# Re-spacing interleaved attention stages, moving partial sums and one late weight sum in a fused attention and expert kernel

## The chip, the cores and the metric

The kernel runs on one core of one Trainium2 chip. The metric is the device time of one execution in microseconds (us), the smaller the better. The granted clock of a run is the mean share of full speed that TensorE was allowed in it; 1.000 means that its profile shows no throttled stretch. TensorE is the matmul engine, VectorE and ScalarE the two elementwise engines, GpSimd the fourth, and the sync engine here only issues DMAs.

## The reference

Four batches of block attention (8 heads, 768 positions, 64 wide, 8 blocks), in which keys and values are first mixed between blocks by a matrix from five rounds of row and column normalization. Then a mixture of four experts over all 3072 tokens.

```python
def _attn_ref(q, k, v, sort_net):
    ...                                   # P: five rounds of exp and normalization of sort_net
    k_sorted = einsum('bhij,bhjcd->bhicd', P, k_b)
    v_sorted = einsum('bhij,bhjcd->bhicd', P, v_b)
    ...                                   # per block: softmax(q k^T / 8) v
def _moe_ref(x, domain_probs, w1, w2):
    p = domain_probs / (domain_probs.sum(-1, keepdims=True) + 1e-09)
    for e in range(E):
        h = np.maximum(x @ w1[e], 0.0)
        out += p[:, e:e + 1] * (h @ w2[e])
```

## The kernel before

The expert part works on chunks of 256 tokens, three to a batch. "Chunk (b, c)" is chunk c of batch b. A chunk has a **first layer** (for each expert 2 x 16 matmuls of 256 columns, each half evicted by VectorE) and a **product part**, seven products of a Strassen-like second layer, each a chain over the experts. The products are named b11, b21, t1, t2, n4, t3 and b22, and need sums of the hidden values (`h_sums`). The six chunks of batches 2 and 3, the **last chunks**, use the seven-product scheme in the first layer too, and their weight sums are prepared in batch 1's chunks.

While the experts of batch 0 run, the attention of batch 1 is computed in between, and batches 2 and 3 follow inside the rest of batch 0 and batch 1. A list says at which chunk and at which place (slot) in it each attention stage is issued:

```python
PLANS = {
    0: [ ...                         # (chunk, slot, stage, batch, pair of heads)
        (2, 7, st_a, 1, 3), (2, 8, st_x, 1, 3), (2, 9, st_v, 2, 0),
        (2, 9, st_q, 2, 0), (2, 10, st_v, 2, 1), (2, 11, st_k, 2, 0), (2, 11, st_lv, 3, 0), (2, 12, st_q, 2, 1),
        (2, 12, st_bk, 2, 1),
    ],
    1: [
        (0, 0, st_s, 2, 0), (0, 0, st_q, 2, 2), (0, 1, st_v, 2, 2), ...
        (1, 11, st_x, 3, 0), (1, 12, st_s, 3, 2), (1, 13, st_s, 3, 3), (1, 13, st_x, 3, 1), (1, 14, st_a, 3, 2),
        (2, 0, st_a, 3, 3), (2, 0, st_x, 3, 2), (2, 2, st_x, 3, 3),
    ],
}
```

Everything on `nc.sync` stands in one queue, in program order: query transposes, the copies of the mixed values, output transposes and the stores of the results.

```python
att = ctx.enter_context(tc.tile_pool(name="att", bufs=2))

def st_v(b, pr):                     # value mix
    ...                              # 2 matmuls, then ScalarE casts into vo
    if pr % 2:
        for r in range(R):           # six copies
            nc.sync.dma_start(vs[...], vo[...])

def st_q(b, pr):                     # query transpose
    qT = att.tile([P, R, P], F16, name=f"qT_{b}_{pr}", tag="qT", bufs=3)
    nc.sync.dma_start_transpose(qT[:], ...)

def st_s(b, pr):                     # scores: 16 matmuls with kT and qT, then 2 exponentials on ScalarE
    ...
def st_a(b, pr):                     # weighted sum, then VectorE normalizes 2 heads
    xsl = att.tile([P, NB, 2, D], F16, name=f"xsl_{b}_{pr}", tag="xsl")[0:BLK]      # 2 buffers
    ...
def st_x(b, pr):                     # output transpose: the input of the experts
    nc.sync.dma_start_transpose(xTs[b][:, pr], xsls[(b, pr)]...)
```

The first layer, and the product part of a last chunk:

```python
def chunk_first(b, c, es, first, slot):
    for e in es:
        for g in range(2):
            ps = psm(...)                                    # 2 buffers
            ...                                              # 16 matmuls
            nc.vector.scalar_tensor_tensor(out=Hb[...], in0=ps[:], ...)     # eviction
            if e > first:
                for w in ((1,), (2, 3))[g]:
                    h_sums(e - 1, w)
            slot()

def last_chunk(...):
    ...
        tt(oa1, bankB, p1[:], ALU.add)
        for e in range(E - 1):
            h_sums(e, 2)
        product(bankC, blk(1, 1), "n4")
        nc.scalar.copy(ob1, bankC)
        h_sums(E - 1, 1)
        h_sums(E - 1, 2)
        for e in range(E):
            h_sums(e, 4)
        product(bankQ, sm(0), "t1")          # needs the first sum of every expert
```

The softmax here doesn't subtract the row's maximum and nothing guards it: scores larger than these inputs give would overflow.

## Time and profile before

| | before |
|---|---|
| time, median of the first 3 runs (range) | 370.25 us (370.07 to 370.59) |
| span of the profiled run | 368.1 us |
| TensorE busy | 356.6 us (97%) |
| granted clock | 0.998 (half rate in the last 1.1 us alone) |

The question is *where* in the span a wait arises, so the most useful view is the table by stretch. Its columns are the stretch, its length, then the busy time and the number of instructions of TensorE, weight loads, VectorE, ScalarE and GpSimd, then the granted clock (1.00 is full), the DMA share and GB/s. I cut it at the first matmul of each chunk. These are chunk 2 of batch 0 and the three chunks of batch 1:

```profile
core 0: us, PE busy (x) PEld busy (x) DVE busy (x) ACT busy (x) POOL busy (x), PEclk, DMA share, GB/s
...
95.98:118.94 22.96, 22.89 (x247) 19.77 (x244) 19.75 (x39) 6.28 (x12) 3.14 (x4) 1.00 1.16 127
118.94:151.31 32.37, 32.06 (x378) 27.77 (x376) 22.31 (x42) 15.59 (x28) 8.82 (x11) 1.00 1.28 162
151.31:185.63 34.32, 33.44 (x400) 28.54 (x398) 26.52 (x50) 18.30 (x32) 0.00 (x0) 1.00 0.60 104
185.63:211.56 25.93, 25.42 (x247) 22.47 (x244) 24.01 (x46) 1.49 (x4) 0.00 (x0) 1.00 0.22 54
```

The first row has hardly a gap: 22.89 of 22.96 us are TensorE. The others leave 0.3 to 0.9 us each.

### The profile page before, as it was taken

How to read it: one execution, taken by the hardware profiler on the slowest of the kernel's cores; microseconds unless marked ns; L12 is line 12 of the kernel's file. 1: busy time of each engine (PE TensorE's matmuls, PEld its weight loads, DVE VectorE, ACT ScalarE, POOL GpSimd, SP SyncE). 2: the span in 40 equal slices, each digit the busy share in tenths (PEclk: the TensorE clock that was granted, in tenths of full speed). 3: DMA queues.
4: the chain of work that ended last, by engine and by line, in shares of the span. 5: the costliest groups of instructions: out<-in, count | busy, mean ns of one | idle time of the engine just before them, and what ended most of it. 6: DMA issues, size and time to landing. Idle time of an engine off the chain costs nothing.

```text
span 368.1 us, 10549 instructions
## 1 busy us (share of the span) xinstructions
PE 356.6 (97%) x4517; PEld 314.3 (85%) x4517; DVE 280.3 (76%) x558; ACT 157.6 (43%) x282; POOL 117.4 (32%) x134
## 2 busy tenths in 40 slices
PE   8799999998999999999999999999999999999996
PEld 8685858877888888878888899899898998998985
DVE  5654798767898686678789769868779679587694
ACT  2664330543233553256510157165283381561740
POOL 8872111841300152000000018137055082180470
PEclk9999999999999999999999999999999999999999
DMA  7999999999998999652750110310301101102101
GB/s 101 207 208 229 209 209 199 202 192 189 184 110 114 189 172 163 126 118 67 81 124 2 57 59 4 57 59 4 86 30 51 67 3 59 60 2 61 57 16 43
DMA packets 69753, 38.34 MB, mean 104 GB/s; under 512 B 40390, under 2 KB 64716, under 8 KB 69708
## 3 DMA queue, kind: packets, MB, share of 16 engines
q0 software_dynamic: 34640, 17.83, 38.5%
q1 hardware_dynamic: 35068, 19.85, 26.4%
q8 instruction: 35, 0.57, 0.6%
q14 instruction: 10, 0.08, 0.1%
HBM read 42.00 MB, written 6.34 MB: 131 GB/s over the span
## 4 chain that ended last, share of the span: by engine, by line
PE 73%; DVE 12%; DMA 7%; ACT 3%; issue 2%; POOL 2%; DVEq 0%; ACTq 0%; POOLq 0%
PE ps_Q L1114 15%; PE ps_h L766 14%; PE ps_p L751 11%; PE ps_X L1025 8%; PE ps_Q L1025 6%; PE ps_Z L1025 5%; DVE Sb L737 4%; PE ps_h L659 3%; DMA arena<-in_v_dram 3%; PE ps_o L694 3%; DMA qT<-arena 2%; DMA arena<-in_q_dram 2%; DVE Sb L739 2%; ACT kT L396 2%; DVE xsl L423 2%
## 5 line engine op out<-in xcount | busy, mean ns | idle before, releaser
L1038 POOL TENSOR_TENSOR Hb<-tmp,pb 128x512 f16<-128x512 f32 x48 | 61.9, 1295 | 153.3 <-ACT tmp L1037 151.3
L766 PE MATMUL ps_h<-xT,w 128*128 128x256 f16 x672 | 78.7, 273 | 0.5 <-DVE Hb L772 0.5
L766 PEld LDWEIGHTS <-w 128*128 128x128 f16 x672 | 64.5, 98 | 9.5 <-issue 0.7
L772 DVE SCALAR_TENSOR_TENSOR Hb<-ps_h,pb 128x1024 f16<-128x1024 f32 x42 | 51.2, 1222 | 17.1 <-PE ps_h L766 17.1
L1025 PEld LDWEIGHTS <-w 128*128 128x128 f16 x768 | 46.6, 98 | 1.0 <-issue 0.3
L1114 PEld LDWEIGHTS <-Sb 128*128 128x128 f16 x384 | 36.7, 98 | 6.7 <-DVE Sb L737 2.7
L1025 PEld LDWEIGHTS <-arena 128*128 128x128 f16 x576 | 34.7, 98 | 0.2
L1037 ACT ACTIVATE tmp<-tmp 128x512 f32<-128x512 f32 x48 | 30.5, 635 | 6.4 <-DVE tmp L1069 5.2
L751 PEld LDWEIGHTS <-Sb 128*128 128x128 f16 x288 | 27.5, 98 | 3.7 <-issue 0.2
L396 ACT CAST kT<-ps_k 64x384 f16<-64x384 f32 x48 | 22.8, 474 | 17.2 <-PE ps_k L387 16.3
L1114 PEld LDWEIGHTS <-Hb 128*128 128x128 f16 x288 | 27.4, 98 | 2.8
L1025 PE MATMUL ps_X<-kT,arena 128*128 128x128 f16 x384 | 29.3, 219 | 0.0
L121 POOL DMA_DIRECT2D arena<-in_q_dram x24 | 19.9, 837 | 25.0 <-DMA qT<-arena 14.9
L1114 PE MATMUL ps_Q<-w,Sb 128*128 128x256 f16 x192 | 25.8, 273 | 1.0 <-DVE Sb L737 1.0
L737 DVE TENSOR_TENSOR Sb<-Hb 128x512 f16<-128x512 f16 x45 | 26.4, 607 | 0.0
L1061 DVE TENSOR_TENSOR tmp<-ps_Q,tmp 128x512 f32<-128x512 f32 x24 | 16.6, 691 | 12.7 <-ACT tmp L1060 8.5
L413 ACT ACTIVATE ET<-ps_s 96x768 f16<-96x768 f32 x24 | 18.1, 802 | 17.9 <-PE ps_s L406 17.8
L1114 PE MATMUL ps_Q<-w,Hb 128*128 128x256 f16 x192 | 23.9, 273 | 0.0
L1045 ACT COPY ps_X<-ps_Z 128x512 f32<-128x512 f32 x24 | 13.7, 570 | 23.1 <-PE ps_Z L1025 22.5
L1114 PE MATMUL ps_Q<-T,Sb 128*128 128x256 f16 x192 | 22.9, 273 | 0.0
L751 PEld LDWEIGHTS <-Hb 128*128 128x128 f16 x216 | 20.4, 98 | 2.9 <-issue 0.3
L1052 ACT COPY tmp<-ps_X 128x512 f32<-128x512 f32 x24 | 14.1, 587 | 12.2 <-PE ps_X L1025 12.2
(188 smaller groups left out, 607.5 us busy)
## 6 DMA issues: line engine op xcount, KB each, us to landing
w<-in_moe_w_dram POOLq DMA_DIRECT2D x7, 1024.0 KB, 27.4
pb<-p_dram SPq DMA_DIRECT2D x12, 512.0 KB, 6.1
arena<-in_k_dram POOLq DMA_DIRECT2D x8, 384.0 KB, 8.3
arena<-in_v_dram POOLq DMA_DIRECT2D x8, 384.0 KB, 8.8
vs<-arena SPq DMA_DIRECT2D x36, 66.0 KB, 5.4
arena<-in_q_dram POOLq DMA_DIRECT2D x24, 96.0 KB, 7.8
out_dram<-ob SPq DMA_DIRECT2D x9, 256.0 KB, 2.0
out_dram<-oa SPq DMA_DIRECT2D x8, 256.0 KB, 2.5
```

Of the source, the lines that this page charges most:

```text
L121: nc.gpsimd.dma_start(t[:, h // 2, :, h % 2, :], q[b, h].rearrange("(t p) d -> p t d", p=P))
L396: nc.scalar.copy(kT[ds(D * hh, D), r], pk[ds(D * r, D), hh].rearrange("p a (i c) -> p a i c", c=CP),)
L413: nc.scalar.activation(ETs[2 * (pr % 2) + hh][:, 0:S].rearrange("c (a x) -> c a x", a=2), pss[hh][0:BLK, :, 0:HS], AF.Exp, bias=0.0, scale ...
L737: tt(sm[0], blk(0, 1), blk(1, 1), ALU.add)
L751: nc.tensor.matmul(ps, lhs(e, f), Ts[e][rhs][:, f, :], start=(first and e == es[0] and f == 0), stop=(done and e == es[-1] and f == KH - 1 ...
L766: nc.tensor.matmul(ps[:, f, :], w1sb[e][:, kc, ds((4 * g + f) * P, P)], xT[:, kc, ds(2 * c * P, 2 * P)], start=(kc == 0), stop=(kc == NKC ...
L772: nc.vector.scalar_tensor_tensor(out=Hb[:, e, ds(4 * g, 4), :], in0=ps[:], scalar=0.0, op0=ALU.max, in1=pb[:, ds(e, 1), :].broadcast_to([P ...
L1025: nc.tensor.matmul(dst[:, ds(f * P, P)], a[lhs][:, k, ds(f * P, P)], t[rhs][:, k, :], start=(first and f == 0 and k == 0), stop=(f == KH - ...
L1037: nc.scalar.activation(src, src, AF.Relu, bias=0.0, scale=1.0)
L1038: nc.gpsimd.tensor_tensor(Hb[:, e, ds(i * KH, KH), ds(j * P, P)], src.rearrange("p (f x) -> p f x", f=KH), pb[:, ds(e, 1), ds(j * P, P)].b ...
L1061: tt(t22, Q, u3, ALU.add)
L1114: nc.tensor.matmul(ps, lhs(e, f), Ts[e][rhs][:, f, :], start=(first and e == 0 and f == 0), stop=(e == E - 1 and f == KH - 1), skip_group_ ...
```

## The change

Its intent is to space the attention stages so that what one stage hands to the next is ready when TensorE gets there, and to take VectorE work out of the places where TensorE waits for VectorE. Four parts, with no instruction added or removed:

1. `PLANS` re-spaced in all chunks from chunk 1 of batch 0 on.
2. In batch 1's chunks the third sums move from the first layer to the product part.
3. In the six last chunks the first sum of expert 3 goes ahead of the second sums.
4. The order of the weight sums, and one more of them (3, 1) left to the first last chunk.

```diff
     PLANS = {
...      (chunk 1 of batch 0)
-            (1, 0, st_q, 1, 1), (1, 0, st_k, 1, 1), (1, 0, st_n, 1, 2), (1, 1, st_s, 1, 0), (1, 2, st_v, 1, 2),
-            (1, 3, st_v, 1, 3), (1, 3, st_q, 1, 2), (1, 3, st_n, 1, 3), (1, 5, st_s, 1, 1), (1, 6, st_a, 1, 0),
+            (1, 0, st_q, 1, 1), (1, 0, st_s, 1, 0), (1, 0, st_n, 1, 2), (1, 1, st_k, 1, 1), (1, 2, st_v, 1, 2),
+            (1, 2, st_q, 1, 2), (1, 3, st_v, 1, 3), (1, 3, st_n, 1, 3), (1, 5, st_a, 1, 0), (1, 7, st_s, 1, 1),
...      (end of chunk 2 of batch 0)
-            (2, 4, st_bv, 2, 1), (2, 4, st_bk, 2, 0), (2, 7, st_a, 1, 3), (2, 8, st_x, 1, 3), (2, 9, st_v, 2, 0),
-            (2, 9, st_q, 2, 0), (2, 10, st_v, 2, 1), (2, 11, st_k, 2, 0), (2, 11, st_lv, 3, 0), (2, 12, st_q, 2, 1),
-            (2, 12, st_bk, 2, 1),
+            (2, 4, st_bv, 2, 1), (2, 4, st_bk, 2, 0), (2, 6, st_v, 2, 0), (2, 7, st_a, 1, 3), (2, 8, st_v, 2, 1),
+            (2, 8, st_q, 2, 0), (2, 9, st_k, 2, 0), (2, 9, st_x, 1, 3), (2, 9, st_bk, 2, 1), (2, 10, st_lv, 3, 0),
+            (2, 10, st_n, 3, 0), (2, 11, st_s, 2, 0), (2, 11, st_q, 2, 1), (2, 12, st_v, 2, 2),
...      (batch 1; nearly every row moves; its last rows:)
-            (1, 11, st_x, 3, 0), (1, 12, st_s, 3, 2), (1, 13, st_s, 3, 3), (1, 13, st_x, 3, 1), (1, 14, st_a, 3, 2),
-            (2, 0, st_a, 3, 3), (2, 0, st_x, 3, 2), (2, 2, st_x, 3, 3),
+            (1, 11, st_a, 3, 1), (1, 11, st_x, 3, 0), (1, 12, st_s, 3, 3), (1, 13, st_a, 3, 2), (1, 13, st_x, 3, 1),
+            (1, 14, st_a, 3, 3), (2, 0, st_x, 3, 2), (2, 1, st_x, 3, 3),
...
-                    for w in ((1,), (2, 3))[g]:
+                    for w in ((1,), (2,) if b else (2, 3))[g]:
...      (and h_sums(e, 3) in the product part of batch 1's chunks, ahead of product t2)
-    A_ORDER = (3, 4, 5, 10, 11, 0, 1, 2, 6, 7, 8, 9)
+    A_ORDER = (6, 7, 8, 0, 1, 2, 3, 4, 5, 9, 10, 11)
...      (last chunk)
-        for e in range(E - 1):
+        h_sums(E - 1, 1)
+        for e in range(E):
             h_sums(e, 2)
         product(bankC, blk(1, 1), "n4")
         nc.scalar.copy(ob1, bankC)
-        h_sums(E - 1, 1)
-        h_sums(E - 1, 2)
...      (PLAN_A: places of the weight sums moved, (2, 13, 3, 1) taken out)
-    late_sums = {(G0, 1): [(3, 2)], (G0, 2): [(3, 3)]}
+    late_sums = {(G0, 1): [(3, 1), (3, 2)], (G0, 2): [(3, 3)]}
```

## The prediction

> **What bounds the kernel now.** I read the page's busy rows first, then the waits of TensorE, then the timeline around each wait, and the DMA issues with their landings last.
>
> ```profile
> PE 356.6 (97%) x4517; PEld 314.3 (85%) x4517; DVE 280.3 (76%) x558; ACT 157.6 (43%) x282; POOL 117.4 (32%) x134
> ...
> PEclk9999999999999999999999999999999999999999
> ```
>
> TensorE is busy for 356.6 of 368.1 us and its granted clock never falls. No instruction is added or removed by the change, only moved, so it can win only what TensorE waits, and it loses wherever it makes TensorE wait. What TensorE waits is in its waits (engine, line, what ended the wait: total us, times, longest):
>
> ```profile
> PE ps_s L406 <- DMA qT<-arena: 1.6, 1, 1.6
> PE ps_R L305 <- DVE sn L293: 1.3, 1, 1.3
> ...
> PE ps_Q L1114 <- DVE Sb L737: 1.0, 6, 0.2
> PE ps_h L766 <- DVE Hb L772: 0.5, 1, 0.5
> PE ps_k L387 <- DVE arena L327: 0.4, 1, 0.4
> PE ps_s L406 <- DVE xsl L423: 0.3, 1, 0.3
> ```
>
> The second line is the prologue, which is not touched. The others are in reach, and all small. Ends of matmuls are modelled, so I also measured from start to start: 12 matmuls of L1114 take 1.31 us (0.109 us each), and a wait then shows 0.15 to 0.2 us longer than in this list.
>
> The repeating wait, in the timeline of one last chunk:
>
> ```profile
> 279.28 2.54 DVE L737 TENSOR_TENSOR Sb<-Hb 128x512 f16<-128x512 f16 x3
> ...
> 282.08 1.08 DVE L739 TENSOR_TENSOR Sb<-Sb,Hb 128x512 f16<-128x512 f16 x3
> ...
> 283.08 0.41 DVE L737 TENSOR_TENSOR Sb<-Hb 128x512 f16<-128x512 f16 x1
> ...
> 283.55 0.61 PE L1114 MATMUL ps_Q<-w,Sb 128*128 128x256 f16 x4 [0.19 <-DVE Sb L737]
> ```
>
> Product t1 begins at 281.89 and wants expert 3's sum at 281.89 + 1.31 = 283.20; the sum stands behind three second sums and comes 0.35 us late.
>
> The stretch where the plan for batch 2 begins, in the timeline:
>
> ```profile
> 115.34 1.21 SPq L375 DMA_TRANSPOSE qT<-arena  x1
> ...
> 115.52 0.49 PE L354 MATMUL ps_v<-arena 128*128 128x384 f16 x2
> ...
> 116.04 0.80 ACT L360 CAST arena<-ps_v 128x768 f16<-128x768 f32 x1 [0.63 <-PE ps_v L354]
> ...
> 116.87 3.78 SPq L368 DMA_DIRECT2D vs<-arena  x6
> ...
> 120.78 0.52 PE L406 MATMUL ps_s<-qT,kT 64*128 64x96 f16 x16
> ...
> 121.46 1.28 SPq L375 DMA_TRANSPOSE qT<-arena  x1
> ```
>
> The first query transpose goes out *before* the second value mix (115.52), whose six copies then occupy the sync queue for 3.8 us. It lands 2.8 us after issue, at 118.1, and scores need it at 120.78.
>
> **What the Trainium skill says.**
> 1. "DMA: Bandwidth & Descriptors", § Queues, rings and completion order: on each DMA engine the descriptors of one issuing queue are consumed in ring order. The trace agrees as far as it shows: the transpose that follows the six copies (121.46) takes 4.7 us to land, the one ahead of them 2.8.
> 2. "SBUF — State Buffer", § Who interferes with whom: a VectorE instruction with two SBUF inputs contends with a GpSimd instruction that reads SBUF. It agrees: L737 takes 2.54/3 = 0.85 us beside GpSimd's L1038, and 0.41 us alone.
> 3. "TensorE: Matmul & The Clock Gate", § Part 1: after an idle window of about 3.4 us TensorE drops to half rate, until it has been busy as long. Nothing here shows it: the longest idle time in the body is 1.6 us and the clock is full.
>
> **The change part by part.**
>
> *Expert 3's first sum ahead (six last chunks).* It runs straight after the add of L1135, near 282.15, done at 282.6, before 283.20. GpSimd's last L1038 ends at 281.55, so it runs alone. The second sums then start 0.4 us later at 0.36 us apiece (1.08/3), first one near 283.0; product t2 wants it at 283.64. Nothing new waits: 6 x 0.35 = **-2.1 us**.
>
> *Batch 1's stages, chunk 1.* Scores of pair 0 move one place up, behind expert 1's first half, where TensorE arrives at 72.0. Their query transpose was issued at 65.79 and takes 7.4 us, so it lands at 73.2, and nothing ahead of it changes: **+1.25**, less a wait of about 0.2 on a key copy at 74.5 that goes. Scores of pair 1 move two places back, past two products: the 1.6 us wait goes, **-1.6**. But the weighted sum now stands two products (2.6 us) ahead of those scores, in the same two PSUM buffers, and VectorE has first to evict (1.22), form two sums (0.7) and normalize two heads (2 x 0.85): free 3.8 us after the weighted sum began, wanted after 3.2, **+0.6**. A wait of 0.2 at 94.7 goes. Together **-0.2**.
>
> *Batch 2's first scores, chunk 2.* This decides. The second value mix and the first query transpose now share a place, mix first. The order listing confirms it: the sync queue holds six copies of vs, then the transpose; and TensorE has these scores three products later, still in this chunk. With t = 0 at the value mix:
> - the cast ends at 1.3 (116.84 - 115.52), the six copies take 3.9 with the change to the transpose (as from 116.87 to 120.75), so it is issued at 5.25;
> - it lands 2.8 to 4.7 later (the two cases above), at 8.0 to 10;
> - until the scores TensorE has the value mix 0.33, t2 1.31, a key mix 0.33, the rest of n4 0.87 and t3 1.31: 4.15 us.
>
> A wait of 3.9 to 5.8 us; as a value load runs beside it, I take **+5.0**. At 2.8 us of landing this is the least it can be.
>
> *Batches 2 and 3, in batch 1's three chunks.* Waits that should go: 0.5 at 142.0 (VectorE), 0.55 at 158.0 (build of the key mix), 0.4 at 160.6, two of 0.3 on ScalarE's key copies at 174 and 178.6, and 0.65 at 192.0, where VectorE had to normalize four heads (4 x 0.85) ahead of two evictions; now two of them come a place earlier. That is -2.7. New: scores follow weighted sums one product apart five times, each catching VectorE's normalize or ScalarE's exponentials (2 x 0.8) by 0.1 to 0.2 us, and 0.2 in two first layers: +1.3. Together **-1.4**.
>
> *Third sums to the product part.* They leave the first layer, where per expert VectorE has 2 x 1.22 + 3 x 0.35 = 3.5 us against TensorE's 32 x 0.109 = 3.5, and go where it idles. Wanted two products (3.5 us) later, four of them take 1.4: no new wait. Its gain is inside the 0.65 above.
>
> *Weight sums.* One more (expert 3's second, 0.68 us, more beside GpSimd) goes into the first last chunk, in front of the add L1061 on which TensorE already waits 0.35 at 221.5: **+0.7**.
>
> *Throttle.* An idle time of 5.0 contains a whole free-running 3.4 us window in (5.0 - 3.4)/3.4, about half, of the cases; half rate for 3.4 us costs 1.7. Estimate from the skill's figure: **+0.8**.
>
> Sum: -2.1 - 0.2 + 5.0 - 1.4 + 0.7 + 0.8 = +2.8, 373.0 us. I take 372.0, because a plan re-spaced like this was probably kept for some gain, and I may have missed waits that it removes.
>
> **Rivals.**
> 1. *The re-spacing pays as meant*: transposes land in time and every listed wait goes: -2.1 - 2.0 - 2.7, near 363.5. Against it: the two query transposes are ordered by the queue, not by TensorE. For it: waits at other places were kept small by the plan before.
> 2. *VectorE becomes the bound in the product parts*: four third sums (1.4 us) among normalizes of 1.7 us and adds of 0.8 in each. Per chunk VectorE has still less than TensorE (28.5 of 40 us from 120 to 160), so a few tenths in each of three chunks: some +0.8 on any of the other outcomes.
> 3. *The long wait swallows others*: while TensorE stands for 5 us, VectorE, ScalarE and the loads catch up, and half of my +1.3 does not happen: 0.5 less. The batch's last output transpose, now behind the query transpose in the queue, hides beside the same wait.
> 4. *The wait throttles the clock*, for longer than one window: 375 to 376.
>
> **Range and chances.** The transpose wait alone spans 3.9 to 5.8, the throttle 0 to 3, the small waits 1.5 either way: 368.3 to 376.0. 2% is 7.4 us. Slower by that needs the full throttle and lost gains, 7%; faster needs that the wait does not exist and unseen gains, 2%.
>
> **What would show it.** In the changed profile: a wait of L406 on the transpose qT of 4 to 6 us near 117, and one of about 1.2 near 72; no wait of L1114 on L737 in the last chunks, and last chunks 0.35 us shorter (25.1 us apart before); a wait near 221 on L1061 of about 1 us; the stretch of batch 1's chunks 0 to 2 shorter by about 1.4 us; perhaps a lower clock in one slice near 120. I am wrong if L406 meets its transpose in time near 117: then the time is 367 or less.

## The result

| | before | after |
|---|---|---|
| time, median of 4 runs (range) | 370.42 us (370.07 to 370.91) | 376.80 us (376.65 to 376.99) |
| span of the profiled run | 368.1 us | 374.6 us |
| granted clock of the runs | 0.998 (profiled run) | 0.986 to 0.991 |

The ratio is 1.0172 (95% interval 1.0154 to 1.0189). A ratio here is the mean time of one kernel's runs over the mean of the other's runs of the same rounds, so it is not quite the ratio of the medians. The changed kernel is slower, by less than 2%. The time is just above the upper end of the predicted range.

The changed line numbers: the first layer is L764 (L766 before), its eviction L770 (L772), the first and second sums L735 and L737 (L737 and L739). Scores (L406), copies (L368), transposes (L375 of the queries, L454 of the outputs) and the last chunks' L1114 kept theirs.

TensorE's waits after (engine, line, what ended the wait: total us, times, longest), and the clock row of its page:

```profile
PE ps_s L406 <- DMA qT<-arena: 5.0, 1, 5.0
PE ps_h L764 <- DVE Hb L770: 2.2, 1, 2.2
...
PE ps_Q L1025 <- DVE tmp L1061: 0.8, 1, 0.8
```

```profile
PEclk9999999999998799999998999999999999999999
```

The waits of before at L1114 are gone, one wait of 5.0 us and one of 2.2 us have come, and the clock dips in two places, slices 13 and 14 and slice 22. In the trace it is at half rate from 118.9 to 125.7 us, which begins inside the first wait, and from 197.4 to 200.8, just behind the second. The same table by stretch as above, cut at the same matmuls of the changed kernel:

```profile
94.98:125.59 30.61, 25.51 (x267) 21.37 (x263) 20.52 (x40) 9.89 (x16) 4.79 (x6) 0.89 1.23 152
125.59:157.18 31.59, 31.57 (x376) 27.80 (x374) 22.80 (x44) 14.07 (x25) 7.21 (x9) 1.00 1.08 140
157.18:190.55 33.37, 33.06 (x405) 28.65 (x402) 24.47 (x47) 17.47 (x31) 0.00 (x0) 1.00 0.45 90
190.55:219.28 28.73, 26.54 (x231) 22.87 (x228) 22.95 (x41) 1.49 (x4) 0.00 (x0) 0.94 0.22 48
```

Put beside the prediction, for every stretch (each length is the difference of the starting times of two first matmuls in the trace):

| stretch | before | after | difference | predicted |
|---|---|---|---|---|
| up to chunk 1 of batch 0 | 70.26 | 70.78 | +0.5 | 0 |
| chunk (0, 1) | 25.72 | 24.20 | -1.5 | -0.2 |
| chunk (0, 2) | 22.96 | 30.61 | +7.65 | +5.8 |
| chunks (1, 0), (1, 1), (1, 2) | 92.62 | 93.69 | +1.1 | -1.4 |
| first last chunk | 26.64 | 26.86 | +0.2 | +0.35 |
| other last chunks and the end | 129.87 | 128.44 | -1.4 | -1.75 |
| sum | 368.07 | 374.58 | +6.5 | +2.8 |

Of the 7.65 us, some 0.8 are work that moved in from chunk (1, 0) (scores of pair 0, 0.45 us, and a value mix, 0.33), so chunk (0, 2) lost 6.9 and batch 1's chunks 1.9.

**The first wait** is the one foreseen. The timeline after:

```profile
112.35 0.50 PE L354 MATMUL ps_v<-arena 128*128 128x384 f16 x2
...
113.71 3.90 SPq L368 DMA_DIRECT2D vs<-arena  x6
...
117.72 1.23 SPq L375 DMA_TRANSPOSE qT<-arena  x1
119.05 1.23 SPq L454 DMA_TRANSPOSE xT<-xsl  x1
...
121.66 0.82 PE L406 MATMUL ps_s<-qT,kT 64*128 64x96 f16 x16 [4.98 <-DMA qT<-arena]
...
122.06 1.73 POOL L121 DMA_DIRECT2D arena<-in_q_dram  x2 [8.16 <-DMA qT<-arena]
```

The six copies hold the sync queue until 117.7, the query transpose goes out behind them and lands at 121.52, 3.8 us later. The 16 score matmuls then take 0.82 us, against 0.52 before: they run at half rate. (The last line, query loads of GpSimd that wait for the same transpose, matters in e1_q_first.)

**The second wait** was not foreseen. The timeline around it:

```profile
188.60 0.35 SPq L815 DMA_DIRECT2D out_dram<-ob  x1
...
189.00 1.26 SPq L454 DMA_TRANSPOSE room<-xsl  x1
...
193.68 0.69 DVE L423 TENSOR_TENSOR xsl<-ps_a,rz 96x512 f16<-96x512 f32 x1 [2.40 <-DMA room<-xsl]
...
195.13 2.34 DVE L770 SCALAR_TENSOR_TENSOR Hb<-ps_h,pb 128x1024 f16<-128x1024 f32 x2
...
196.39 3.94 PE L764 MATMUL ps_h<-xT,w 128*128 128x256 f16 x22 [2.19 <-DVE Hb L770]
```

Read it backwards. TensorE waits at 196.39 for an eviction, because both buffers of the first layer are full. VectorE evicts late (195.13) because ahead of the evictions in its program stands the normalize of the last weighted sum (batch 3, pair 3), which waits 2.40 us. It waits for a *buffer*: there are two xsl tiles, and pair 3 takes the one of pair 1, which is free only when pair 1's output transpose (189.00) has read it, at 193.59. That transpose stands in the sync queue behind the store of a result (188.60), which in its turn waits for the last add of product t3. Before the change this weighted sum stood one place later in the plan, in the first layer of the next chunk.

In the last chunks, product t1 no longer waits. The timeline after, for comparison with the one in the prediction:

```profile
289.50 1.91 PE L1114 MATMUL ps_Q<-w,Sb 128*128 128x256 f16 x16
289.67 0.41 DVE L735 TENSOR_TENSOR Sb<-Hb 128x512 f16<-128x512 f16 x1
...
290.00 1.42 DVE L737 TENSOR_TENSOR Sb<-Sb,Hb 128x512 f16<-128x512 f16 x4
```

All 16 matmuls run in one row, the sum of expert 3 comes at 289.67, right behind the add, and the four second sums follow.

### The profile page after: what moved, and what is told of

Same layout as the page of the kernel before. It is cut to its first block, busy times and chain, and to the rows that moved or that the text cites. A ratio compares the mean times of both kernels' runs of the same rounds, so it can differ in the third digit from the quotient of the medians. Undisturbed runs are those within 1.5% of the kernel's fastest.

```text
span 374.6 us, 10552 instructions
## 1 busy us (share of the span) xinstructions
PE 358.7 (96%) x4517; PEld 317.2 (85%) x4517; DVE 279.9 (75%) x558; ACT 157.6 (42%) x282; POOL 118.0 (31%) x134
## 4 chain that ended last, share of the span: by engine, by line
PE 82%; DMA 7%; DVE 4%; POOL 2%; issue 2%; ACT 2%; SPq 0%; DVEq 0%; ACTq 0%; POOLq 0%
PE ps_Q L1114 20%; PE ps_h L764 19%; PE ps_p L749 11%; PE ps_X L1025 7%; PE ps_Q L1025 5%; PE ps_Z L1025 5%; DMA w<-in_moe_w_dram 4%; PE ps_h L657 3%; PE ps_o L692 3%; PE ps_p L799 2%; PE ps_s L406 2%; DMA room<-xsl 1%; DMA arena<-in_v_dram 1%; PE ps_v L354 1%; POOL Hb L1038 1%
## 5 line engine op out<-in xcount | busy, mean ns | idle before, releaser
L764 PE MATMUL ps_h<-xT,w 128*128 128x256 f16 x672 | 80.1, 276 | 2.2 <-DVE Hb L770 2.2
L764 PEld LDWEIGHTS <-w 128*128 128x128 f16 x672 | 65.4, 99 | 11.9 <-issue 2.7
L770 DVE SCALAR_TENSOR_TENSOR Hb<-ps_h,pb 128x1024 f16<-128x1024 f32 x42 | 51.2, 1222 | 20.5 <-PE ps_h L764 20.3
L1114 PEld LDWEIGHTS <-Sb 128*128 128x128 f16 x384 | 37.2, 98 | 4.1
L749 PEld LDWEIGHTS <-Sb 128*128 128x128 f16 x288 | 28.0, 100 | 4.0
L1114 PEld LDWEIGHTS <-Hb 128*128 128x128 f16 x288 | 27.4, 98 | 2.9
L735 DVE TENSOR_TENSOR Sb<-Hb 128x512 f16<-128x512 f16 x45 | 26.5, 609 | 0.0
L1114 PE MATMUL ps_Q<-w,Sb 128*128 128x256 f16 x192 | 24.7, 273 | 0.0
L1114 PE MATMUL ps_Q<-w,Hb 128*128 128x256 f16 x192 | 23.9, 273 | 0.0
L1114 PE MATMUL ps_Q<-T,Sb 128*128 128x256 f16 x192 | 22.9, 273 | 0.0
```

Source lines behind the costliest of these rows:

```text
L735: tt(sm[0], blk(0, 1), blk(1, 1), ALU.add)
L749: nc.tensor.matmul(ps, lhs(e, f), Ts[e][rhs][:, f, :], start=(first and e == es[0] and f == 0), stop=(done and e == es[-1] and f == KH - 1 ...
L764: nc.tensor.matmul(ps[:, f, :], w1sb[e][:, kc, ds((4 * g + f) * P, P)], xT[:, kc, ds(2 * c * P, 2 * P)], start=(kc == 0), stop=(kc == NKC ...
L770: nc.vector.scalar_tensor_tensor(out=Hb[:, e, ds(4 * g, 4), :], in0=ps[:], scalar=0.0, op0=ALU.max, in1=pb[:, ds(e, 1), :].broadcast_to([P ...
L1114: nc.tensor.matmul(ps, lhs(e, f), Ts[e][rhs][:, f, :], start=(first and e == 0 and f == 0), stop=(e == E - 1 and f == KH - 1), skip_group_ ...
```

## The experiments

**Theory.** The loss comes from two places where something that TensorE needs hangs on a transpose far back in the sync queue, and from the half rate that follows each wait; the rest of the change gains. **Rivals.** VectorE is loaded too much by the moved sums; or the gains elsewhere exist only because the other engines catch up during the long wait. Each experiment was timed in five rounds with the kernel before on the same chip (six runs with the profiled one; five for e3_both and four for f1_recombined); the medians of before were 370.63 us (first four kernels), 370.94 (next four) and 370.75 (last four).

| kernel | median us (range) | ratio to before (95%) | span of the profiled run |
|---|---|---|---|
| e1_q_first | 377.68 (375.03 to 379.35) | 1.0190 (1.0152 to 1.0229) | 374.3 |
| e2_a33_back | 374.31 (372.92 to 374.74) | 1.0092 (1.0067 to 1.0116) | 372.3 |
| e3_both | 374.58 (374.00 to 376.15) | 1.0108 (1.0080 to 1.0135) | 372.5 |
| e4_sum_ahead | 368.81 (368.15 to 370.04) | 0.9954 (0.9930 to 0.9977) | 368.0 |
| e5_v_later | 373.93 (372.04 to 374.87) | 1.0075 (1.0046 to 1.0104) | 370.7 |
| e5_warm | 372.36 (371.73 to 374.02) | 1.0041 (1.0017 to 1.0065) | 370.3 |
| e6_x31 | 373.74 (372.17 to 374.40) | 1.0064 (1.0041 to 1.0087) | 371.7 |
| e7_third_sums | 370.85 (370.18 to 372.88) | 0.9998 (0.9973 to 1.0023) | 368.3 |
| f1_recombined | 366.84 (366.27 to 367.34) | 0.9894 (0.9878 to 0.9910) | 364.4 |
| f2_chunk1_sum | 367.45 (367.21 to 368.47) | 0.9917 (0.9903 to 0.9931) | 365.4 |
| f3_old_plans | 368.97 (368.83 to 370.66) | 0.9962 (0.9945 to 0.9980) | 366.8 |
| f4_warm_x31 | 371.79 (371.24 to 373.39) | 1.0034 (1.0016 to 1.0051) | 370.3 |

### e1_q_first: the query transpose ahead of the copies

```diff
 (changed kernel, end of chunk 2 of batch 0)
-            (2, 8, st_v, 2, 1), (2, 8, st_q, 2, 0),
+            (2, 8, st_q, 2, 0), (2, 8, st_v, 2, 1),
```

> The changed kernel with one pair of stages swapped within its place: batch 2's first query transpose goes out before the second value mix, so ahead of its six copies in the sync queue. Theory (queue order): the 5.0 us wait of L406 on qT near 117 goes, and with it the half-rate clock after it (about 1.7 us): 6 to 6.7 us off the changed kernel, about 370.4 us. Rival (the transfers are slow because a value load runs beside them, whatever the order): the transpose still lands 4 us or more after the scores want it; 375 us or more.

Measured: no gain, 377.68 us. The query transpose wait shrank to 1.42 us, and another took its place, as its timeline shows:

```profile
110.47 1.50 SPq L375 DMA_TRANSPOSE qT<-arena  x1
...
118.73 1.24 SPq L454 DMA_TRANSPOSE xT<-xsl  x1
118.85 0.52 PE L406 MATMUL ps_s<-qT,kT 64*128 64x96 f16 x16 [1.42 <-DMA qT<-arena]
119.25 1.73 POOL L121 DMA_DIRECT2D arena<-in_q_dram  x2 [4.61 <-DMA qT<-arena]
...
126.05 1.23 PE L764 MATMUL ps_h<-xT,w 128*128 128x256 f16 x5 [4.61 <-DMA xT<-xsl]
```

The output transpose of batch 1's last pair is still behind the six copies (issued 118.73, landed 126.01), and the first layer of the next chunk needs it. In the changed kernel its landing (122.31) was hidden beside the longer wait, as the third rival of the prediction had it. The theory was incomplete: the six copies stand ahead of *two* transposes that TensorE needs soon.

The order in the queue is not all of it, and the expectation's rival (slow in any order) is partly right here. The query transpose, out at 110.47 and so ahead of the copies, took 8.2 us to land. And the output transpose stands at the same place as in the changed kernel (issued 119.05 there), but took 7.28 us instead of 3.3. The trace shows what went beside it: GpSimd's next query loads wait for the query transpose, which came earlier, so they went out at 119.25 instead of 122.06, and 1097 of their packets ran during this landing. In e3_both there were 1597 and it took 5.95 us; in the changed kernel, e2_a33_back and e6_x31 there were 0 to 14 and it took 3.3 to 3.8. How much of the 4.6 us comes from the queue and how much from these loads was not separated by a run.

### e2_a33_back: the last weighted sum back in its old place

```diff
 (changed kernel, batch 1)
-            (1, 14, st_a, 3, 3), (2, 0, st_x, 3, 2),
+            (2, 0, st_a, 3, 3), (2, 0, st_x, 3, 2),
```

> The changed kernel with the last weighted sum (batch 3, pair 3) back at its place of before, one place later. Theory (its normalize waits for an xsl buffer whose transpose is still in flight, 2.4 us on VectorE, and two evictions stand behind it): the 2.2 us wait of L764 on L770 near 196 goes, and the half-rate clock after it (about 1.6 us): 3 to 4 us off the changed kernel, about 373.3. Rival (VectorE is overloaded there by the weight sums and the moved third sums): the wait stays at over 1 us; 375.5 or more.

Measured: 374.31 us, the ratio 0.8 percentage points lower than the changed kernel's, about 3 us. The second wait falls from 2.2 to 0.5 us and its clock dip is gone; the first wait (5.2 us) and its dip stay. So this one move cost the second wait.

### e3_both: both of these

> Both of the above in one kernel. If the two waits are all that the change loses, the two gains add: 9.5 to 10.5 us off the changed kernel, 366.3 to 367.3, so 3 to 4 us under the kernel before. If there is a third loss that they cover, it stays above 368.5.

The edit is the two above together. Measured: 374.58 us, as e2 alone within the intervals; the wait for the output transpose (4.6 us) is again there in place of the one for the query transpose. The expectation failed for the reasons that e1 had shown.

### e4_sum_ahead: the last chunks' sums alone, on the kernel before

```diff
 (kernel before, last chunk)
+        h_sums(E - 1, 1)
-        for e in range(E - 1):
+        for e in range(E):
             h_sums(e, 2)
         ...
-        h_sums(E - 1, 1)
-        h_sums(E - 1, 2)
```

> The kernel before with one part of the change alone: in the six last chunks expert 3's first sum runs ahead of the second sums. Theory: six waits of 0.35 us go, 2.0 to 2.1 us off the kernel before, 368.2 to 368.4, ratio 0.9945. Rival: another sum is then late instead (VectorE does the same work in the same time), under 0.7 us gained.

Measured: 368.81 us, ratio 0.9954. In its trace all six waits at L1114 are gone and the last chunks are 24.74 us apart, 25.07 to 25.10 before. Six times 0.35 is the 2.1 us predicted; the timed gain is 1.7, with an interval from 0.9 to 2.6. (The span of its profiled run, 368.0, hides this: that run, the slowest of the six, had a half-rate stretch in the prologue, from 14.0 to 20.8 us, behind a wait of 2.3 us that the change does not touch.)

### e5_v_later: the six copies behind both transposes

```diff
 (changed kernel, end of chunk 2 of batch 0)
-            (2, 8, st_v, 2, 1), (2, 8, st_q, 2, 0),
+            (2, 8, st_q, 2, 0),
 ...
-            (2, 10, st_lv, 3, 0),
+            (2, 10, st_v, 2, 1), (2, 10, st_lv, 3, 0),
```

> The changed kernel with the second value mix of batch 2 two places later, so that in the sync queue the query transpose and the output transpose of pair 3 both go ahead of its six copies. The swap alone moved the wait from the query transpose (5.0 us) to the output transpose (4.6 us). Theory (both transposes were behind the copies, and the copies are what the queue spends its time on): no wait over 1.5 us is left between 105 and 135, and the clock stays full there: 5.5 to 6.7 us off the changed kernel, about 370.5. Rival (the queue drains its bytes by about 121.5 in any order, so somebody waits for it): a wait of over 3 us appears on the copies vs, on ScalarE's value copy or on the next query transpose; 374 or more.

Measured: 373.93 us. Both transpose waits are gone, which confirms that the queue's order made them, and the chunk (0, 2) is 24.2 us long instead of 30.6 (with the scores in it). The query transpose, out at 109.76, landed at 116.96, just before the scores. But a third wait comes. Its timeline:

```profile
124.54 0.80 ACT L360 CAST arena<-ps_v 128x768 f16<-128x768 f32 x1 [5.34 <-DMA vs<-arena]
125.39 0.48 PE L354 MATMUL ps_v<-arena 128*128 128x384 f16 x2 [2.21 <-ACT arena L360]
```

The next value cast overwrites what the six copies read, so it waits until they have landed. The next value mix waits for that cast, 2.2 us. So the time is the rival's (374 or more), and the wait on the copies is one that it had named. The six copies have a reader in front, a writer behind and two transposes beside them, and the changed plan has them in too narrow a place whichever way they stand. This profiled run has no half rate behind its wait at 125 and has it behind the one at 192.

### e5_warm: the wait kept, the throttle taken away

```diff
 (changed kernel, st_s)
         pss = [psa([P, 2, 512], F32, f"ps_s_{b}_{pr}_{hh}") for hh in range(2)]
+        if (b, pr) == (2, 0):
+            for _ in range(80):
+                nc.tensor.matmul(pss[0][:, 0, 0:P], ident[:], ident[:], start=True, stop=True)
```

These matmuls write to a bank that the scores then overwrite, so the result stays right. They need no data that is late.

> The changed kernel with 80 extra 128-column matmuls (identity by identity, their result is overwritten) in front of batch 2's first scores, so that TensorE works through about 4.5 of the 5 us that it waits. The transpose still lands when it did. Theory (idle time itself lets the clock fall to half rate): scores start when they did, near 121.7, but the clock stays full behind them, 1.5 to 2.0 us off the changed kernel, about 375.0. Rival (the half-rate stretch comes from something else, such as the power of the burst after the wait): the clock falls anyway, no gain.

Measured: 372.36 us, more than expected. Its timeline at the first wait:

```profile
116.81 4.63 PE L406 MATMUL ps_s<-ident 128*128 128x128 f16 x80
...
122.74 0.52 PE L409 MATMUL ps_s<-qT,kT 64*128 64x96 f16 x16 [1.31 <-DMA qT<-arena]
```

The scores begin as late as ever, when the transpose has landed (122.70), but at full rate. From their first matmul to the first layer of the next chunk it takes 2.10 us (122.74 to 124.84), where the changed kernel takes 3.93 (121.66 to 125.59): the half rate costs **1.8 us** there. The clock is 1.000 in five of its six runs.

The rest of its gain was unexpected: its second wait is only 0.4 us. The order of the queue is the same (store at 187.78, transpose 0.40 us later), but the transpose landed in 2.84 us, where in the changed kernel it took 4.59.

### e6_x31: one transpose ahead of a store

```diff
 (changed kernel, batch 1)
-            (1, 12, st_s, 3, 3), (1, 13, st_a, 3, 2), (1, 13, st_x, 3, 1),
+            (1, 12, st_x, 3, 1), (1, 12, st_s, 3, 3), (1, 13, st_a, 3, 2),
```

> The changed kernel with the output transpose of batch 3's pair 1 one place earlier, ahead of the store of the second output tile in the sync queue; the last weighted sum stays early. Theory (VectorE's normalize waits for that transpose because it stood behind the store, which waits for an add): the transpose goes out near 185 instead of 189 and has landed when the normalize of pair 3 begins; the waits of 2.4 us on VectorE and 2.2 us on TensorE near 196 go, and the half-rate clock behind them: 3 to 4 us off the changed kernel, as with the weighted sum put back. Rival (the early weighted sum itself overloads VectorE): at most 1.5 us off.

Measured: 373.74 us; the ratio is 1.1 percentage points below the changed kernel's, which is 3 to 4 us, as expected. Its timeline:

```profile
186.69 1.22 SPq L454 DMA_TRANSPOSE room<-xsl  x1
...
190.03 0.35 SPq L815 DMA_DIRECT2D out_dram<-ob  x1
...
194.20 1.21 DVE L770 SCALAR_TENSOR_TENSOR Hb<-ps_h,pb 128x1024 f16<-128x1024 f32 x1
```

The transpose now goes 3.3 us ahead of the store, its buffer is free in time, and neither the second wait nor its clock dip appears. The weighted sum stays where the change put it. Nothing but one line's place in a queue is different. Chunks (1, 1) and (1, 2) take 33.36 + 24.72 = 58.1 us here, 60.25 before and 62.1 in the changed kernel: the re-spacing makes these chunks 2.2 us shorter, of which 0.5 is a weighted sum that it moves into chunk (1, 0), and the wait with its half rate took 4.0.

(A third xsl buffer, the other way to free the normalize, does not fit in memory, so that kernel does not build and was not run.)

### e7_third_sums: the third sums alone, on the kernel before

```diff
 (kernel before, chunk_first and the product part of batch 1's chunks)
-                    for w in ((1,), (2, 3))[g]:
+                    for w in ((1,), (2,) if b else (2, 3))[g]:
 ...
+            for e in es:
+                h_sums(e, 3)
             times(bankA, sm(1), "t2", es, False)
```

> The kernel before with one part of the change alone: in batch 1's chunks the third sums leave the first layer and run in the product part. Theory: VectorE had no wait of TensorE there but the one near 192 (0.65 us), and the sums are wanted 3.5 us after they run; between 0 and 0.8 us off the kernel before, ratio 0.998 to 1.000. Rival: four more sums among the normalizes make scores wait for their buffers, up to 1 us slower.

Measured: 370.85 us, ratio 0.9998. Batch 1's three chunks take 32.37, 34.32 and 25.87 us, 32.37, 34.32 and 25.93 before. No gain and no cost: the rival that VectorE becomes the bound in the product parts is out for the old plans. For the new ones e6_x31 speaks against it: in its trace no wait of TensorE in these chunks is longer than 0.21 us.

### f3_old_plans: everything but the plans

This is the changed kernel with both `PLANS` as they were before.

> The changed kernel with the plans of batches 0 and 1 as they were before: all of the loss should be in the plans, so this keeps the sum ahead (-1.7) and the extra late weight sum (+0.6) and nothing else: 369.5, ratio 0.997. Rival (third sums and weight sums in the product part load VectorE): over 371, ratio over 1.001.

Measured: 368.97 us, ratio 0.9962. All of the loss is in the plans; the other three parts together gain 1.4 us. The first last chunk is 26.87 us long in its trace, and 26.30 in e4, which lacks the extra late weight sum: that sum costs 0.57 us.

### f2_chunk1_sum: chunk 1's re-spacing and the sum ahead

This is e4 with the ten rows of chunk 1 of batch 0 as the change has them.

> The kernel before, with two parts of the change alone: the re-spaced stages of batch 1 in chunk 1 of batch 0, and expert 3's first sum ahead. If the 1.5 us that chunk 1 is shorter by in the changed kernel's trace are the re-spacing's own: 370.6 - 1.7 - 1.5 = 367.4, ratio 0.991. As the prediction had it (chunk 1 wins 0.2 us, the new wait at the first scores eats the rest): 368.7, ratio 0.995.

Measured: 367.45 us, where e4 had 0.9954 the ratio is 0.9917. The chunk is 24.21 us long, 25.72 before. So its 1.5 us are the re-spacing's own and do not hang on the long wait that comes later. The wait that the prediction feared at the first scores of this chunk varies from run to run with the landing of the transpose: of the runs with the re-spaced chunk it is none in the changed kernel, here and in three others, 0.2 to 0.6 us in four, and 1.25 in one (f4).

### f4_warm_x31: two remedies together

This is the changed kernel with the edits of e5_warm and e6_x31.

> The changed kernel with both remedies already tried: 80 matmuls that keep TensorE busy ahead of the late query transpose, and the output transpose of batch 3's pair 1 one product earlier. In its profile the run with the 80 matmuls had the second wait too only 0.4 us long, because that transpose landed in 2.8 us instead of 4.6. If that landing was a gift of that run, both remedies together take away 1.7 of half rate and 3.1 of the second wait with what follows it: 376.8 - 1.7 - 3.1 = 372.0 on a chip where before is 370.6, so about what the 80 matmuls alone gave (372.4). If the remedies are separate and each keeps its measured gain (4.4 and 3.1): 369.3.

Measured: 371.79 us, ratio 1.0034, little better than e5_warm (1.0041), far from 369.3. So the two gains are not separate: most of e5_warm's extra gain is the second wait, which e6_x31 takes away for certain. Why the transpose landed faster in the run with the 80 matmuls was not tested. Five of its six timed runs have a clock of 1.000, so it was probably not that one run's luck alone, but those runs have no trace. The traces have a candidate, the fetch of instructions (last section): the 80 matmuls shift it, and none fell beside this transpose.

### f1_recombined: a version that beats both

The changed kernel with the start of batch 2's attention put back in front of the copies, x31 as in e6, and the late weight sum (3, 1) back in its old place:

```diff
 (changed kernel, end of chunk 2 of batch 0)
-            ... (2, 6, st_v, 2, 0), (2, 7, st_a, 1, 3), (2, 8, st_v, 2, 1), (2, 8, st_q, 2, 0), ...
-            ... (2, 9, st_x, 1, 3), ... (2, 11, st_s, 2, 0), (2, 11, st_q, 2, 1), (2, 12, st_v, 2, 2),
+            ... (2, 7, st_a, 1, 3), (2, 8, st_x, 1, 3), (2, 9, st_v, 2, 0), (2, 9, st_q, 2, 0),
+            (2, 10, st_v, 2, 1), (2, 11, st_k, 2, 0), (2, 11, st_lv, 3, 0), (2, 12, st_q, 2, 1), (2, 12, st_bk, 2, 1),
 (batch 1, chunk 0: scores of pair 0 at place 0, third value mix at 1, the stages up to place 9 re-spaced to fit)
 (batch 1, chunk 1: st_x of batch 3's pair 1 at place 12; PLAN_A with (2, 13, 3, 1), late_sums without it)
```

> The changed kernel with the start of batch 2's attention put back where it was before the change (output transpose of pair 3 and first query transpose ahead of the second value mix, first scores at the start of batch 1's first chunk), the output transpose of batch 3's pair 1 one product earlier, and the extra late weight sum back in its old place. My theory (the change's loss is the two waits at sync-queue transposes and the half rate behind them, and the rest of the re-spacing is worth 1.5 us in chunk 1 and about 2 in batch 1's later chunks, and the sum ahead 1.7 to 2.1): 370.6 - 1.7 - 1.5 - 2.2 = about 365, ratio 0.985, and no wait of TensorE over 1 us behind the prologue. Rival (what the re-spacing won elsewhere depends on the long wait, in which the other engines catch up): 367.5 to 369, with new waits in batch 1's first chunk.

Measured: 366.84 us (366.27 to 367.34), ratio 0.9894: 1.1% faster than before, and by the two ratios (0.9894 over 1.0172) 2.7% faster than the changed kernel. No wait over 1.1 us is left in its profile. The timeline at the critical place:

```profile
114.92 1.21 SPq L375 DMA_TRANSPOSE qT<-arena  x1
...
116.45 3.80 SPq L368 DMA_DIRECT2D vs<-arena  x6
...
120.36 0.51 PE L406 MATMUL ps_s<-qT,kT 64*128 64x96 f16 x16
```

It is 1.8 us short of what was expected. Chunks (1, 0) to (1, 2) take 91.5 us, 1.1 less than before instead of 2.2: chunk (1, 0) is 1.1 us longer, half of it stages moved in from the next one and half new waits of 0.3 and 0.35 us. To that extent the rival was right. f2, a far smaller edit, gets within 0.6 us of it.

## Why the prediction was wrong

The direction, the main mechanism and the place were right; the time was 376.8 us, 0.8 above the range.

1. **The wait at batch 2's first scores: right.** Predicted 5.0 us out of 3.9 to 5.8, measured 4.98. (That 5.0 is the least at a landing of 2.8 us is a slip: 5.25 + 2.8 - 4.15 is 3.9.) The chain holds link by link: issue 5.25 us after the value mix, measured 5.37 (112.35 to 117.72); landing between 2.8 and 4.7, measured 3.8. e5_v_later and f1_recombined show that the order in the queue makes it.
2. **The throttle: right in kind, too small.** Predicted +0.8 as a chance of one half times 1.7. It happened at the long wait in all five profiled runs with a wait of 4.6 to 5.5 us there, and cost 1.8 (e5_warm). It came a second time, behind the wait that I had not foreseen: 16 matmuls at 0.213 us apart instead of 0.109, 1.7 us. The skill's page, "TensorE: Matmul & The Clock Gate", § Part 1, says that half rate follows an idle window of about 3.4 us; I took this as a window that must lie wholly inside the wait. The second wait is 2.19 us long, so that reading is wrong: in the traces a window that was idle for about half of its length was enough (last section).
3. **Batches 2 and 3 in batch 1's chunks: the step that failed.** Predicted -1.4, measured +1.9 after allowing for the 0.8 us that moved out. The prediction looked at this very place ("0.65 at 192.0, where VectorE had to normalize four heads ahead of two evictions; now two of them come a place earlier") and counted it as a gain. It asked when the normalize can start on VectorE, and not which buffer it writes: one of two, freed by a transpose behind a store in the sync queue. e2_a33_back and e6_x31 show that. The wait was as long as 2.2 us because that transpose took 4.59 us to land; with 2.84 at the same place of the program, e5_warm had 0.4 left. Without the wait and its half rate the change gains 1.7 in chunks (1, 1) and (1, 2) (e6) and 0.5 in chunk (1, 0), moved stages taken out: 2.2, more than predicted.
4. **Chunk 1 of batch 0: mis-sized.** Predicted -0.2, measured -1.5 (f2 has the same). The term of +1.25 for a new wait at the first scores was worked out from one landing time, 7.4 us; it took 6.7 in the changed kernel, TensorE came 0.5 us later, and there was no wait. In other profiled runs the wait was 0 to 1.25.
5. **The sum ahead: right.** -2.1 predicted, 2.1 in the traces, 1.7 timed (e4).
6. **Third sums: right**, zero (e7). **The late weight sum: about right**, +0.7 predicted, +0.57 measured (f3 beside e4).
7. **The shading: wrong.** My sum was 373.0, and I took 1.0 off it because such a plan "was probably kept for some gain". Nothing in the profile said so. The range had the same fault: its own terms (a wait of 5.8, a throttle of 3, small waits of 1.5) add up to about 377.5, not 376.0.

Point by point, from +2.8 to +6.5: chunk 1 better by 1.3; chunk (0, 2) worse by 1.1 beyond its moved work; batch 1's chunks worse by 3.2; last chunks and the start worse by 0.7.

## What to carry to other kernels

A transfer is as late as what stands in front of it in its queue: before moving a stage, list what its queue holds up to the next few things that the busiest engine needs, and check both ends, who waits for the data and who waits for the buffer that the transfer still reads. Taking one late transfer out shows the next (e1), so move the block that delays them, not the one that complains, and look which loads an earlier landing will set going beside the next transfer. And count a wait of two microseconds of TensorE as possibly four: what follows it may run at half rate.

## What the Trainium skill lacked or had wrong

- "TensorE: Matmul & The Clock Gate", § Part 1, has half rate after at least one idle window of about 3.4 us; how much of the window has to be idle it does not say. In the runs part of it was enough. The changes of the clock in each trace lie whole multiples of 3.41 us apart. Cut into windows at these times, every window at full rate in which TensorE was idle for 59% or more ended in half rate (64% twice in the changed kernel, 59% in e5_v_later at 192), and none of 43% or less did. Between them lie 48% (e4_sum_ahead, in the prologue: half rate) and 47.5% (e7_third_sums at 84: full rate). So these runs put the limit near a half, with ends of matmuls that are modelled. It follows that a wait of 2.2 us can go either way. Of five of 2.2 to 2.3 us, three were followed by half rate (the changed kernel at 196, e5_v_later at 192, e4_sum_ahead at 12) and two were not, since a border cut them (e1 at 198 into 1.43 and 0.75 us, e5_v_later at 125 into 0.99 and 1.22). All five waits of 4.6 to 5.5 us were, and none of 0.8 to 2.0.
- No page that I read has the spread of landings of one and the same small transpose. Issued 0.4 us behind a store, with no load of GpSimd beside it, it landed in 2.8 to 2.9 us 18 times in the fourteen traces, in 4.4 to 4.8 us 11 times and in 3.4 to 3.5 us 3 times. The traces show what went with it: the DMA view has a queue of kind "instruction", 35 packets of 16 KB in a run (36 with the 80 extra matmuls). In all 11 slow landings such a packet began 0.7 to 2.5 us after the transpose was issued; in 17 of the 18 fast ones none began before it had landed (the other is f3_old_plans at 184.9). In the changed kernel one began at 191.4, beside the transpose of 189.00 (4.59 us); in e5_warm none began between 183.8 and 195.0, and the transpose of 188.18 took 2.84. No experiment moved these packets on purpose, so this is a companion and not a cause that was shown; 1.7 us of a tuned plan hang on it.
